# Two pairs of heads turned by transposing transfers instead of TensorE, in a MoBA attention and GELU MLP kernel

## The chip, the cores and the metric

The kernel runs on one core of a Trainium2 chip. A core has a matmul engine (TensorE; PE in the profile, and PEld for its loads of weights), three engines for elementwise work (VectorE: DVE; ScalarE: ACT; GpSimd: POOL) and SyncE (SP), which here does nothing but issue transfers. Each engine runs its own list of instructions in order and waits on semaphores for what others produce. The metric is device time in microseconds (us) for one execution, and lower is better.

## What is computed

```python
# q, k, v: (4, 8, 768, 64) f32; blocks of 64 positions, 12 blocks, top 3
k_rep = k.reshape(B, H, 12, 64, D).mean(axis=3)
gate = einsum('bhsd,bhnd->bhsn', q, k_rep)      # later blocks: -1e9
# each row sees its own block and the 3 blocks with the highest gates
scores = where(mask & causal, q @ k.T / 8, -1e9)
attn = softmax(scores)
x = (attn @ v)  ->  (4 * 768, 8 * 64)           # tokens x model
h = x @ w_in                                    # (3072, 512) @ (512, 2048)
out = gelu_tanh(h) @ w_out                      # (2048, 512) -> (3072, 512) f32
```

## The kernel before

**Work and stages.** All matmuls take fp16 operands. The 8 heads of a batch are handled in pairs: `HP = 4` pairs per batch, 16 pairs in all, and pair `p` belongs to batch `p // 4`. For a pair, `load` fetches k, q and v through SyncE's queue (the first piece as one operation, the others as a second one). `pre(p)` turns k and q so that the head dimension lies on partitions (for `p >= 4` a DVE stream transpose, L585), computes the gates (TensorE, L699), picks the three best blocks (DVE, L715 to L736) and puts the mask's rows beside q. Up to pair 7 TensorE turns the mask; from pair 8 on a transposing transfer on SyncE does so (L776). `heads(p)` then computes scores (L1059), exponentials (ACT, L1072), the causal cut (POOL, L1086), the product with v (L1098), and a division by the row sum (`norm`, DVE, L981 and L982) that writes the fp16 tile `xn` with tokens on partitions. There are three `xn` buffers. Batch 0 has a form of its own, `heads2`.

For the MLP a batch's attention output must lie with the model dimension on partitions, in `xT2[b % 2]`, one row of 128 partitions for each pair. That is the work of `turn_out(p)`, and it has two forms:

- **by TensorE**: six 128x128 transposes (`ot_e`, L1001) into one PSUM bank, and one copy from there into `xT2` (`otc_e`, through `copy`: L365 where ACT runs it, L369 where DVE does);
- **by transfer**: one `dma_start_transpose` on SyncE (`ot_dma`, L1006) from `xn` into `xT2`, with no other engine.

Before the change the second form is used by pairs 6, 8, 9, 10, 12, 13 and 14, the first one by all others. The last pair of each batch (3, 7, 11, 15) is always turned by TensorE.

Per batch, `s1` expands (L1135, GELU at L1147) and a second stage contracts: batch 0 plainly (`s2_plain`, L1335), the later batches by a seven-product scheme (`s2`, L1385, with sums at L1322 and joins at L1434 on DVE). The last batch also has a seven-product expansion (`s1_seven`, L1224). The stages overlap: while TensorE contracts batch 0, it also runs the heads of batch 1 and the preparation of batch 2, and so on.

**What sets the order.** The body builds a list of operations with `add`: the engines that may run each, its emitter, and what it depends on. Three tables written out in the file then decide the schedule. `ORDER` is the sequence in which operations are emitted, so that each engine's list is the part of `ORDER` that belongs to it. `BUFFER` picks the buffer for each operation that takes one. `ENGINE` holds the exceptions to "the first engine named". Nothing is reordered afterwards: SyncE's queue in particular is in order, so a transfer that waits for its data holds back the loads, masks and stores queued behind it.

**Fillers.** `warm` has 72 small matmuls on zeros (L1537) that compute nothing; `ORDER` contains 34 of them, most in the first microseconds.

Of the kernel before, what the change touches and what calls it, by code (L numbers as in the profile page):

```python
# [181 lines left out]
    "DVE": [  # L182
        2, 56, 61],
    "POOL": [
        338, 586, 587, 646, 647, 707, 708, 972, 973, 1035, 1036, 1097, 1098,
        1159, 1160, 1426, 1488, 1550, 1551]}


# [1451 lines left out]
```

## Time and profile before

| | us |
|---|---|
| median of 3 runs | 251.6 |
| the runs | 251.35, 251.6, 251.69 |
| the profiled execution, its own time | 252.62 |
| its span in the profile | 250.9 |
| PE busy | 245.2 |
| PEld busy | 170.7 |
| DVE busy | 194.9 |
| ACT busy | 173.8 |
| POOL busy | 82.2 |

The profiled execution is 1.0 us above the median of the runs, and 1.7 us of its time lies outside the span. Its mean granted TensorE clock was 0.997. Engine busy times are those of one profiled execution. Matmuls are pipelined, so one matmul's recorded duration overlaps the next one's, and a busy PE isn't PE at its peak. In rows of the timeline the columns are: start, duration, engine, line, operation, output and input, and xN for N instructions in a row.

### The profile page before, as it was taken

To read this page: it belongs to the slowest core of one execution; us is meant where nothing else is said; L and a number is where in the kernel's file an instruction comes from. 1 tells how busy PE (TensorE), PEld (TensorE's weight loads), DVE (VectorE), ACT (ScalarE), POOL (GpSimd) and SP (SyncE) were. 2 spreads that over 40 slices of the span, in tenths; PEclk is the share of its full clock that TensorE was granted. 3 is DMA by queue.
4 is the path that set the end of the run, shared out by engine and by line. 5 is a ranking of instruction groups with operands and counts; after the bars stand their busy time and mean duration, and the time that the engine had idled before them with its cause. 6 is when DMAs were issued, how large, how long until landed. Compare 5 with 4: busy or idle time off the path is not lost.

```text
span 250.9 us, 6484 instructions
## 1 busy us (share of the span) xinstructions
PE 245.2 (98%) x2504; PEld 170.7 (68%) x2504; DVE 194.9 (78%) x551; ACT 173.8 (69%) x220; POOL 82.2 (33%) x161
## 2 busy tenths in 40 slices
PE   8999999999999999999999999999999999999993
PEld 6768686555555666555788887656777887666883
DVE  3799971060989899999997999999788587788944
ACT  2788886635699997779997885586899932667200
POOL 8466660001147485080156351400256600000000
PEclk9999999999999999999999999999999999999998
DMA  6997899999897828999999486105813430020023
GB/s 181 229 203 158 138 210 186 211 172 161 156 172 125 160 47 153 177 234 195 205 191 186 74 155 109 26 3 135 206 44 37 108 114 0 3 84 0 3 105 146
DMA packets 128878, 32.61 MB, mean 130 GB/s; under 512 B 121456, under 2 KB 124880, under 8 KB 128848
## 3 DMA queue, kind: packets, MB, share of 16 engines
q1 hardware_dynamic: 125136, 27.62, 54.9%
q0 software_dynamic: 3136, 4.19, 9.9%
q10 hardware_dynamic: 576, 0.39, 0.6%
q8 instruction: 19, 0.31, 0.5%
q14 instruction: 11, 0.09, 0.2%
HBM read 27.26 MB, written 6.29 MB: 134 GB/s over the span
## 4 chain that ended last, share of the span: by engine, by line
PE 94%; DVE 4%; issue 0%; DVEq 0%
PE wide L1135 27%; PE bank L1385 22%; PE wide L1059 11%; PE bank L1335 8%; PE bank L1098 6%; PE wide L1224 6%; PE wide L876 3%; PE bank L699 2%; PE bank L1537 2%; PE bank L944 2%; PE bank L1001 1%; PE bank L565 1%; PE bank L558 1%; PE bank L769 1%; DVE sel L731 1%; DVE sel L722 1%
## 5 line engine op out<-in xcount | busy, mean ns | idle before, releaser
L1135 PE MATMUL wide<-xT,w_in 128*128 128x384 f16 x416 | 75.0, 326 | 0.0
L1072 ACT ACTIVATE ats<-wide 128x896 f16<-128x896 f32 x72 | 62.3, 915 | 5.9 <-PE wide L1059 4.6
L1147 ACT ACTIVATE G<-wide 128x768 f16<-128x768 f32 x52 | 41.8, 808 | 28.2 <-PE wide L1135 25.8
L1135 PEld LDWEIGHTS <-w_in 128*128 128x128 f16 x416 | 39.8, 98 | 25.9 <-issue 0.8
L1086 POOL TENSOR_SCALAR_AFFINE_SELECT ats<-ats 128x256 f16<-128x256 f16 x72 | 31.4, 448 | 64.6 <-ACT ats L1072 61.8
L1059 PE MATMUL wide<-qT,kT 76*128 76x512 f16 (+3 forms) x192 | 38.4, 305 | 0.0
L1385 PE MATMUL bank<-w_out,G 128*128 128x256 f16 x216 | 33.7, 272 | 0.0
L1385 PEld LDWEIGHTS <-G 128*128 128x128 f16 x288 | 26.7, 98 | 6.4
L585 DVE STREAM_TRANSPOSE s<-sd 128x768 f32<-128x768 f32 x24 | 23.3, 973 | 9.3 <-DMA sd<-in_k_dram 8.8
L1335 PE MATMUL bank<-w_out,G 128*128 128x512 f16 x96 | 29.2, 379 | 0.0
L1098 PEld LDWEIGHTS <-ats 128*128 128x128 f16 x504 | 22.7, 98 | 4.5 <-issue 0.3
L1434 DVE TENSOR_TENSOR osb<-bank,osb 128x512 f32<-128x512 f32 (+1 forms) x38 | 22.2, 594 | 4.4 <-PE bank L1385 3.0
L1098 PE MATMUL bank<-v,ats 128*128 128x65 f16 x504 | 24.9, 194 | 0.0
L1059 PEld LDWEIGHTS <-kT 76*128 76x128 f16 x192 | 17.3, 97 | 10.4 <-issue 0.6
L895 ACT ACTIVATE ats<-wide 128x1024 f16<-128x1024 f32 (+3 forms) x24 | 20.9, 919 | 3.1 <-PE wide L876 3.1
L1385 PEld LDWEIGHTS <-XS 128*128 128x128 f16 x216 | 20.1, 97 | 4.2 <-DVE XS L1322 0.2
L1385 PE MATMUL bank<-TS,XS 128*128 128x256 f16 x144 | 22.1, 272 | 0.0
L367 POOL CAST v<-vsd 128x768 f16<-128x768 f32 x12 | 10.3, 863 | 31.9 <-DMA vsd<-in_v_dram 31.8
L367 POOL CAST kT<-s 64x768 f16<-64x768 f32 x19 | 16.3, 862 | 9.3 <-DVE s L585 8.0
L982 DVE TENSOR_TENSOR xn<-bank,zr 128x384 f16<-128x384 f32 x24 | 13.4, 558 | 0.8
L731 DVE MAX8 sel<-sel 128x8 f32<-128x12 f32 x160 | 13.3, 157 | 0.6
L365 ACT CAST qT<-s 64x768 f16<-64x768 f32 x15 | 12.4, 825 | 0.2
(126 smaller groups left out, 356.2 us busy)
## 6 DMA issues: line engine op xcount, KB each, us to landing
out_dram<-osb SPq DMA_DIRECT2D x23, 256.0 KB
vsd<-in_v_dram SPq DMA_DIRECT2D x26, 192.0 KB
sd<-in_k_dram SPq DMA_DIRECT2D x48, 96.0 KB
sd<-in_q_dram SPq DMA_DIRECT2D x48, 96.0 KB
w_in<-in_moe_w_in_dram POOLq DMA_DIRECT2D x2, 1024.0 KB, 11.2
w_out<-in_moe_w_out_dram POOLq DMA_DIRECT2D x2, 1024.0 KB, 13.5
G<-in_k_dram SPq DMA_DIRECT2D x4, 192.0 KB
G<-in_q_dram SPq DMA_DIRECT2D x4, 192.0 KB
```

Of the source, the lines that this page charges most:

```text
L367: nc.gpsimd.tensor_copy(out=out, in_=in_)
L585: nc.vector.transpose(out=T[key + "T32", p], in_=T[key, p].rearrange("p t j -> p (t j)"))
L895: nc.scalar.activation(out=T["at", u][:, :, 0:n], in_=plan.buf[("st",) + u].rearrange("p (h w) -> p h w", h=2)[:, :, 0:n], func=AF.Exp, bi ...
L1059: nc.tensor.matmul(st[:, x:e], kT16[i][h][0:76, s0:s0 + 128], qT16[i][h][0:76, s0 + (x - cb):s0 + (e - cb)], start=True, stop=True)
L1072: nc.scalar.activation(out=T["at", u][:, 0:n], in_=plan.buf[("st",) + u][:, 0:n], func=AF.Exp, bias=0.0, scale=SCALE)
L1086: nc.gpsimd.affine_select(out=dg, in_=dg, compare_op=ALU.is_ge, fill=0.0, base=0, pattern=[[0, 2], [1, 128]], channel_multiplier=-1)
L1098: nc.tensor.matmul(pvv[:, qc, 0:65], at[:, cb + (qc - jc) * 128: cb + (qc - jc + 1) * 128], v16[i][:, jc, h, :], start=(gi == 0 and jc == ...
L1135: nc.tensor.matmul(hps[:, 512 * e:512 * e + HALF], w_in16[:, ci, (2 * j + e) * 128: (2 * j + e + 1) * 128], T["xT", b][:, ci, HALF * h:HAL ...
L1147: nc.scalar.activation(out=G[:, :, h, j, :], in_=plan.buf["hps", b, j, h].rearrange("p (e w) -> p e w", e=2)[:, :, 0:HALF], func=AF.Gelu_a ...
L1335: nc.tensor.matmul(plan.buf["ops", b, ti], G[:, f % 2, 2 * ti // NC, f // 2, ti % (NC // 2) * 128:ti % (NC // 2) * 128 + 128], w_out16[:, ...
L1385: nc.tensor.matmul(dst[:, HD * h:HD * h + HD], FACT[m][0][:, j, t * 128:(t + 1) * 128], FACT[m][1][:, j, :], start=(clear and j == 0), sto ...
L1434: nc.vector.tensor_tensor(out=dst(), in0=src(), in1=other(), op=ALU.add)
```

## The change

The condition in `turn_out` now admits all pairs of batch 1 but its last, so that pairs 4 and 5 take the second form too. The three tables were searched anew for this program. Because a turn by transfer adds three operations to the list where the turn by TensorE adds two, operation numbers shift by one behind pair 4's turn and by two behind pair 5's; the tables are therefore wholly replaced.

```diff
@@ turn_out @@
-        if p >= HP + 2 and hp != HP - 1:
+        if p >= HP and hp != HP - 1:
             go = add({SP: 1.3}, ot_dma, norms, -50)
             x = [add({"DMA": 0.8}, lambda _: None, [go], base - 20,
                      lag=2.0)] * 2
@@ ORDER, around the turns of pairs 4, 5 and 6 @@
...
-    662, 517, 665, 678, 715, 707, 663, 713, 714, 518, 579, 643, 519, 679,
...
-    1033, 673, 970, 685, 627, 527, 736, 724, 528, 628, 529, 743, 1036, 739,
...
+    686, 725, 737, 687, 974, 733, 529, 627, 1036, 530, 741, 730, 1026, 706,
+    531, 579, 688, 532, 738, 734, 745, 726, 544, 1027, 628, 739, 533, 689,
...
@@ ORDER, the last warm matmuls (1922 up to 1925) @@
...
-    1922, 784, 548, 1045, 785, 796, 1158, 786, 825, 450, 549, 826, 827, 828,
...
-    1098, 852, 1923, 853, 1473, 1002, 854, 821, 990, 1003, 487, 855, 856,
...
+    305, 1924, 1925, 294, 163, 317, 310, 326, 318, 306, 319, 328, 295, 153,
+    363, 364, 329, 311, 365, 315, 366, 358, 320, 356, 367, 324, 359, 149,
...
```

In the old numbers 579 and 627 are pair 4's and pair 5's transposes on TensorE, 580 and 628 the copies behind them (pair 4's on DVE, pair 5's on ACT), and 687 pair 6's transfer. In the new numbers 579, 628 and 689 are the transfers of pairs 4, 5 and 6; 627 and 688 are the second divisions of pairs 5 and 6, so pair 6's first and pair 5's second division change places on DVE. 1026 and 1027 are the two load operations of pair 9's q. SyncE's list around them, read out of the two tables:

| before | after |
|---|---|
| q of pair 9, first piece | q of pair 9, first piece |
| q of pair 9, others | **turn of pair 4** |
| q of pair 10, first | q of pair 9, others |
| k of pair 10, first | **turn of pair 5** |
| turn of pair 6 | turn of pair 6 |
| q of pair 10, others | k of pair 10, first |
| k of pair 11, first | q and k of pair 11, first |
| k of pair 10, others | q of pair 11, others |
| q of pair 11, first | v of pair 9, first |
| v of pair 9, first | k of pair 10, others |
| k of pair 11, others | an output store |
| v of pair 8, first | k of pair 11, others |
| v of pair 9, others | q of pair 10, first |
| mask of pair 8 | an output store |
| | q of pair 10, others |
| | v of pair 8, first |
| | mask of pair 8 |

The number of warm matmuls stays at 34. Before, two of them (1922 and 1923) lie in the expansion of batch 1; after, all of them stand ahead of the first expansion matmul of batch 0 (363). Operations that change their engine: in the first 36 us several copies, casts and turns move between DVE, ACT and POOL, in both directions, and ACT's first table load moves behind ACT's first loads and its first copy; in the last batch's expansion and contraction four copies and one sum move from DVE to ACT.

More of the change, by code (lines that the diff above doesn't have):

```diff
@@ L21 @@
 ORDER = [
[128 rows of a table removed]
-BUFFER = [
[23 rows of a table removed]
[128 rows of a table added]
+BUFFER = [
[23 rows of a table added]
 ENGINE = {
     "ACT": [
[4 rows of a table removed]
[5 rows of a table added]
     "DVE": [
-        2, 56, 61],
+        5, 56, 145],
     "POOL": [
-        338, 586, 587, 646, 647, 707, 708, 972, 973, 1035, 1036, 1097, 1098,
-        1159, 1160, 1426, 1488, 1550, 1551]}
+        337, 587, 588, 648, 649, 709, 710, 974, 975, 1037, 1038, 1099, 1100,
+        1161, 1162, 1427, 1428, 1552, 1615]}
 class Op:
```

303 rows, old and new, of tables (BUFFER, ENGINE, ORDER) are left out of this document.

## The prediction

> **What bounds the kernel now.** I read the busy times and the chain's shares first, to find the engine, then busy times by stretch, to see where that engine is without a gap, then the waits in the stretch where the two turns lie.
>
> ```profile
> span 250.9 us, 6484 instructions
> PE 245.2 (98%) x2504; PEld 170.7 (68%) x2504; DVE 194.9 (78%) x551; ACT 173.8 (69%) x220; POOL 82.2 (33%) x161
> ...
> PE 94%; DVE 4%; issue 0%; DVEq 0%
> ```
>
> TensorE is busy for 98% and is 94% of the chain. A share over the whole span doesn't say where work taken from it is worth its time, so here are four stretches (columns: length; busy time and instructions of PE, PEld, DVE, ACT, POOL; granted clock; DMA share; GB/s): batch 0's attention, the contraction of batch 0 with the heads of batch 1 in it, the expansion of batch 1, and the last batch's expansion.
>
> ```profile
> 0.00:36.00 36.00, 34.24 (x525) 25.63 (x526) 28.57 (x124) 26.70 (x37) 24.01 (x56) 1.00 0.92 186
> 62.00:98.50 36.50, 36.50 (x395) 21.60 (x395) 32.36 (x101) 32.72 (x42) 20.14 (x37) 1.00 0.77 134
> 98.50:121.00 22.50, 22.50 (x156) 13.11 (x155) 21.85 (x81) 17.62 (x24) 5.10 (x6) 1.00 0.98 198
> 204.00:231.00 27.00, 26.97 (x189) 18.25 (x188) 21.41 (x32) 14.89 (x18) 0.00 (x0) 1.00 0.10 40
> ```
>
> Up to 36 us TensorE has 1.76 us of gaps. In the second stretch, where pairs 4 and 5 are turned, and in the third it has none, and the clock is full. Idle time of DVE there (4.14 of 36.50) is nobody's bound. Of the waits in 62.00 to 98.50, TensorE itself has no row; its loads of weights have seven, first and last:
>
> ```profile
> PEld bank L699 <- issue: 0.7, 2, 0.4
> ...
> PEld L1001 <- DVE xn L982: 0.3, 1, 0.3
> ```
>
> Such a load waits while the matmul before it still runs, so none of them opens a gap. The end is set by how much TensorE has to issue behind the first stretch; what leaves its list there should come off the end, if nothing else becomes late.
>
> **Part 1: twelve transposes leave TensorE.** Pair 4's and pair 5's, with the matmul behind each:
>
> ```profile
> 86.01 0.50 PE L1001 MATMUL bank<-ident,xn 128*128 128x128 f16 x6
> 86.34 0.38 PE L1335 MATMUL bank<-w_out,G 128*128 128x512 f16 x1
> ...
> 91.96 0.50 PE L1001 MATMUL bank<-ident,xn 128*128 128x128 f16 x6
> 92.29 0.81 PE L1335 MATMUL bank<-w_out,G 128*128 128x512 f16 x3
> ```
>
> The recorded 0.50 overlaps the matmul that follows, so the cost in the stream is from start to start: 86.34 − 86.01 = 0.33, and 92.29 − 91.96 = 0.33. Both lie in a stretch without gaps: **−0.66 us**, bounded above by the recorded 2 × 0.50 = 1.00 and below by nothing, if the gap is filled by another wait.
>
> **Part 2: two copies go, three transposing transfers now stand in one row on SyncE.** All tiles written into `xT2`, grouped (count: shortest/median/longest in ns, first and last start):
>
> ```profile
> L369 DVE COPY xT<-bank x7: 349/551/558, 31.9 to 203.2; 128x768 f16<-128x768 f16 x5, 128x384 f16<-128x384 f16 x2
> L1006 SPq DMA_TRANSPOSE xT<-xn x7: 1212/1377/2127, 93.0 to 199.4; - x7
> L365 ACT COPY xT<-bank x3: 793/798/799, 92.8 to 154.0; 128x768 f16<-128x768 f16 x3
> ```
>
> A copy of 0.55 leaves DVE and one of 0.80 leaves ACT. Both engines have more idle time than that between 62.00 and 98.50, so I cost these at nothing: they are slack for others, not path. Each new transfer takes SyncE 1.2 to 2.1 us, median 1.38. Where do they fit? SyncE's list around the turn of pair 6, and the third of the last four divisions of pairs 5 and 6 (DVE, L982), which is pair 6's first in the old order and pair 5's second in the new one:
>
> ```profile
> 84.38 2.92 SPq L411 DMA_DIRECT2D sd<-in_q_dram  x5
> 87.34 0.76 SPq L411 DMA_DIRECT2D sd<-in_k_dram  x1
> 92.97 1.34 SPq L1006 DMA_TRANSPOSE xT<-xn  x1
> 94.36 1.70 SPq L411 DMA_DIRECT2D sd<-in_q_dram  x3
> ...
> 103.77 1.36 SPq L776 DMA_TRANSPOSE mT<-madd  x1
> ```
> ```profile
> 90.75 0.56 DVE L982 TENSOR_TENSOR xn<-bank,zr 128x384 f16<-128x384 f32 x1
> ```
>
> SyncE issues nothing from 87.34 + 0.76 = 88.10 to 92.97: it waits for pair 6's second division. Pair 4's data is complete before 86.01, when it is turned today; its transfer comes behind the first of the loads that begin at 84.38 and doesn't wait. Pair 5's second division, third in the new order, ends at 90.75 + 0.56 = 91.31; its transfer then takes 91.31 to about 92.69, and pair 6's can start at 92.97 as before. So the two new transfers fill a hole of 4.87 us in SyncE's list, and pair 6's turn isn't delayed by issue time.
>
> Are they in time? The expansion of batch 1 reads the four pairs in turn:
>
> ```profile
> 95.85 0.49 PE L1135 MATMUL wide<-xT,w_in 128*128 128x384 f16 x2
> ...
> 98.54 0.65 PE L1135 MATMUL wide<-xT,w_in 128*128 128x384 f16 x3
> ```
>
> Pair 4's row is needed at 95.85, some 9 us behind its issue; pair 5's at about 97, 5.7 behind; pair 6's no earlier than 98.54. TensorE waits for nothing there today, so pair 6's transfer, issued at 92.97, has landed within 98.54 − 92.97 = 5.6 us or a little more. With at most that for pair 5's, it lands by 91.31 + 5.6 = 96.9, which is just when it is needed, and this is an upper bound. Cost taken: 0.
>
> The wait of pair 5's turn holds back what is queued behind it on SyncE: pair 6's turn and then the first pieces of pair 10's k, pair 11's q and pair 11's k, three more of q 11, and so on; pair 10's q moves to the end of that row. Nothing on TensorE waits directly; DVE's stream transposes (L585) do. Its first use of that row today is at
>
> ```profile
> 99.97 0.97 DVE L585 STREAM_TRANSPOSE s<-sd 128x768 f32<-128x768 f32 x1
> ```
>
> and takes pair 10's q, whose last pieces were issued by 94.36 + 1.70 = 96.06: 3.9 us ahead. In the new order pair 11's q takes that place; its last piece is the sixth behind pair 6's turn, at 1.70 / 3 = 0.57 each: 94.36 + 6 × 0.57 = 97.8, which leaves 2.2 us, 1.7 less. The other three of the group keep more than 4 us, worked out in the same way. DVE didn't wait for a load at that place, so landing takes at most 3.9 us; how much less the trace of before doesn't show. I take 0 and price the other case below.
>
> **Part 3: two warm matmuls leave the expansion of batch 1** (they go ahead of 36 us, where TensorE has gaps).
>
> ```profile
> 109.84 0.27 PE L1537 MATMUL bank<-XS 128*128 128x256 f16 x1
> 109.95 0.33 PE L1135 MATMUL wide<-xT,w_in 128*128 128x384 f16 x1
> ...
> 121.74 0.27 PE L1537 MATMUL bank<-XS 128*128 128x256 f16 x1
> ```
>
> Start to start 0.11, twice: **−0.22 us**, and the two take 0.22 us of the 1.76 us of gaps in the first stretch.
>
> **Part 4: other engines for some copies and a table load, at the two ends.** In the first stretch two of the moves bear on TensorE's gaps.
>
> ```profile
> 1.76 1.28 ACT L842 ACT_TABLE_LOAD   x1 [1.76 <-PEq L1624]
> ...
> 5.97 0.68 ACT L365 COPY s<-bank 128x384 f32<-128x384 f32 x1 [2.72 <-PE bank L565]
> 7.45 1.71 ACT L365 CAST XS<-bank 128x384 f16<-128x384 f32 x2 [0.80 <-DVE ks L604]
> ```
> ```profile
> 21.54 1.01 DVE L369 COPY s<-bank 128x384 f32<-128x384 f32 x2
> ```
>
> The two copies at 21.54 (1.01 us) go from DVE to ACT; if DVE's chain sets the first stretch, that is worth up to −1.0. The table load (1.28) goes behind the copy that ends at 5.97 + 0.68 = 6.65; it then ends at 7.93, while the casts behind it start at 7.45 today: up to +0.5. I take 0, between the two, since each needs its engine to be the bound at that place and the chain has only 4% of DVE. In the last batch's expansion DVE has 21.41 and ACT 14.89 of 27.00, so a few copies moved from one to the other fit in either: 0, within ±0.5.
>
> **Sum.** −0.66 − 0.22 = −0.88 us. Against the profiled execution's own 252.62: 251.7. That execution was 1.0 us above the median of the runs shown; the edits don't depend on what made it so, and 251.6 − 0.9 = **250.7 us** for the median.
>
> **The rivals.**
> - *The gain is given back.* The first stretch costs up to 0.5 and the last expansion up to 0.5, and together they eat the 0.88: **251.6**. For it: all three tables are different, and parts outside the turns are moved. Against: both places have idle time on the engines that get more. The Trainium skill's "Perfetto Trace Analysis", in Identifying the Most-Contended Engine, says that matmul busy time is a poor measure of TensorE's headroom and that the busy share of weight loads is the better one. By that rule 68% would be slack, and the gain 0. The trace speaks against it at this place: starts follow each other without a gap, and no row names TensorE as waiting.
> - *Slower: loads held back on SyncE.* Pair 11's q is issued 1.7 us closer to its stream transpose. If landing takes the full 3.9 us, DVE stands still for 1.7 us at about 100 us, in a stretch where it is busy for 21.85 of 22.50 and can make up only 0.65; what it prepares there are the masks and sums of batch 1's contraction. It decides once a landing takes longer than 2.2 us by more than that 0.65. Undiminished on TensorE, it costs 1.7: 250.7 + 1.7 = **252.4**. For it: DVE's share there, and a DMA share of 0.98. Against: DVE's list is also in a new order, and some of its work could be done first.
> - *Slower by far: the transfers run one after another.* If the 5.6 us of pair 6's turn are transfer time and not latency, and the queue does one at a time, pair 5's would run 91.31 to 96.9 and pair 6's 96.9 to 102.5, while it is needed from 98.54 on, at about 98.9 (one matmul later): 3.6 us late, 250.7 + 3.6 = **254.3**. Against: SyncE starts a new piece 1.4 us behind a turn, and the 5.6 is only an upper bound. The Trainium skill's "VectorE: DVE Perf Modes" speaks for it, and against the change: under The three transpose paths and Rules for kernel authors it gives 1309 ns for 128x128 by DMA against 390 ns on TensorE, and advises TensorE wherever PSUM will do as a destination. By it six blocks would take 7.9 us, an estimate from that page; the trace disagrees, since 5.6 us were enough for pair 6's six.
> - *The order also shortens the first stretch*, by the 1.0 us of part 4: **249.7**.
>
> **How the numbers follow.** The forecast (250.7, own range 250.2 to 251.2, from ±0.5 at either end of the kernel) gets 0.55, since it needs only that work leaves an engine without gaps. Gain given back: 0.17. Loads late: 0.18. Transfers in series: 0.04. Shorter first stretch: 0.06. A run of this kernel can tell 0.2% or 0.5 us from no change. Faster by more: 0.53 of the forecast's 0.55 and the last rival's 0.06, 0.59; the same: 0.17 and the 0.02 left, 0.19; slower: 0.22. The range 249.8 to 252.4 reaches to the late loads and leaves out the transfers in series and half of the last rival's cases.
>
> **What the changed profile would show.** Right: six transposes by TensorE in seven groups instead of nine, nine L1006 transfers, three of them between 85 and 95 us; no wait of TensorE between 62 and 121 us; PE busy down by about 0.7 to 0.9; the first expansion matmul (L1135) still at about 36.5. Part 4 is wrong if that first L1135 moves by more than 0.3. The late loads would show as DVE idle before L585, released by a DMA, at about 100 us, and as PE busy below its stretch between 98 and 145 us. Transfers in series would show as a gap of TensorE before L1135 near 98 us, released by a DMA into xT. The forecast is wrong if PE loses its 0.9 us and the end doesn't move: then the rows of waits between 121 and 250 us must show who gave it back.

## The result, and the profile after

| | before | after |
|---|---|---|
| median, 12 runs of each | 251.83 us | 251.3 us |
| lowest and highest | 251.35 to 252.4 | 250.97 to 251.91 |
| the profiled execution, its own time | 252.62 | 251.68 |
| its span | 250.9 | 250.0 |

The ratio of after to before is 0.9977, 95% interval 0.9966 to 0.9987: the change is faster by 0.53 us of the medians, where 0.88 was forecast. A second set of 12 runs of the same kernel (e8 below) gave 251.25 and a ratio of 0.9975 (0.9959 to 0.999).

The page of the profile after, its span, busy times and chain:

```profile
span 250.0 us, 6442 instructions
PE 244.1 (98%) x2492; PEld 170.0 (68%) x2492; DVE 189.0 (76%) x542; ACT 178.1 (71%) x226; POOL 81.0 (32%) x162
...
PE 90%; DMA 5%; DVE 3%; ACT 0%; issue 0%; POOL 0%; DVEq 0%
```

Twelve matmuls fewer, and something new in the chain: 5% of a DMA. The busy times by stretch (columns as in the prediction; the second row, from 36 to 62 us, is the expansion of batch 0) say where it is. The kernel before in that second stretch, and then the changed kernel in all four:

```profile
36.00:62.00 26.00, 26.00 (x182) 15.37 (x179) 5.96 (x11) 14.82 (x20) 2.46 (x4) 1.00 1.14 184
```
```profile
0.00:36.00 36.00, 34.24 (x527) 25.48 (x527) 27.98 (x122) 27.71 (x39) 23.79 (x57) 1.00 0.92 183
36.00:62.00 26.00, 25.64 (x185) 14.94 (x183) 5.29 (x10) 14.31 (x19) 2.51 (x4) 1.00 1.16 186
62.00:98.50 36.50, 36.50 (x383) 21.67 (x376) 34.41 (x103) 33.16 (x42) 20.03 (x37) 1.00 0.78 139
98.50:121.00 22.50, 22.50 (x166) 13.54 (x165) 20.56 (x79) 16.51 (x23) 3.94 (x4) 1.00 1.03 203
```

From 62 us on TensorE still has no gap. Between 36 and 62 it lost 0.36 us that it did not lose before. Its timeline at the first contraction matmul, before and after:

```profile
46.27 0.81 PE L1135 MATMUL wide<-xT,w_in 128*128 128x384 f16 x4
46.92 0.38 PE L1335 MATMUL bank<-w_out,G 128*128 128x512 f16 x1
```
```profile
44.60 0.65 PE L1136 MATMUL wide<-xT,w_in 128*128 128x384 f16 x3
45.61 0.38 PE L1336 MATMUL bank<-w_out,G 128*128 128x512 f16 x1 [0.36 <-DMA w_out<-in_moe_w_out_dram]
45.83 0.48 PE L1136 MATMUL wide<-xT,w_in 128*128 128x384 f16 x2
```

The first contraction matmul has ten expansion matmuls fewer ahead of it than before (48 instead of 58). It wants to start at 45.25 and waits for the first half of w_out. Before, it started at 46.92 without a wait.

The turns. SyncE's list, and the tiles written into `xT2`:

```profile
86.80 1.33 SPq L1007 DMA_TRANSPOSE xT<-xn  x1
88.19 1.70 SPq L412 DMA_DIRECT2D sd<-in_q_dram  x3
92.13 2.76 SPq L1007 DMA_TRANSPOSE xT<-xn  x2
94.95 0.57 SPq L412 DMA_DIRECT2D sd<-in_k_dram  x1
95.57 0.52 SPq L412 DMA_DIRECT2D sd<-in_q_dram  x1
96.13 0.52 SPq L412 DMA_DIRECT2D sd<-in_k_dram  x1
96.70 1.66 SPq L412 DMA_DIRECT2D sd<-in_q_dram  x3
```
```profile
L1007 SPq DMA_TRANSPOSE xT<-xn x9: 1209/1211/1330, 86.8 to 198.9; - x9
```

Nine transfers, three of them ahead of batch 1's expansion, which begins at 96.07; pair 4's runs without waiting, pair 5's waits for its division until 92.13, pair 6's follows at once. TensorE waits for none of them, and its transposes are down from 54 to 42, as forecast.

For the accounting I use two landmarks of each trace: the start of the first expansion matmul, and the time from there to the last matmul's start. Before they are 36.51 and 210.22, after 36.30 and 209.65. Each ratio in the table is to runs of the kernel before that were timed beside that kernel; their medians were 251.81 to 251.93.

| kernel | median | ratio to before (95%) | first expansion matmul | from there to the last matmul |
|---|---|---|---|---|
| before | 251.83 | | 36.51 | 210.22 |
| after | 251.3 | 0.9977 (0.9966 to 0.9987) | 36.30 | 209.65 |
| e1_turns_only | 251.7 | 1.0001 (0.9987 to 1.0014) | 35.63 | 209.89 |
| e2_order_only | 252.13 | 1.0012 (1.0 to 1.0024) | 35.55 | 210.33 |
| e3_contract_later | 250.95 | 0.997 (0.9957 to 0.9984) | 35.91 | 209.29 |
| e4_ten_warm | 252.52 | 1.0032 (1.002 to 1.0045) | 36.28 | 210.39 |
| e5_turns_filled | 251.25 | 0.9977 (0.9963 to 0.9992) | 35.24 | 209.81 |
| e6_two_more_turns | 263.32 | 1.0457 (1.0432 to 1.0482) | 42.48 | 215.34 |
| e7_pair7_turn | 251.5 | 0.9984 (0.997 to 0.9997) | 35.60 | 210.08 |
| e8_changed_again | 251.25 | 0.9975 (0.9959 to 0.999) | 36.19 | 209.13 |
| e9_two_fillers_off | 250.59 | 0.9947 (0.9928 to 0.9967) | 35.63 | 209.14 |
| e10_contract_later_again | 250.87 | 0.9961 (0.9947 to 0.9974) | 36.17 | 209.30 |
| e11_old_two_fillers_off | 251.4 | 0.9982 (0.9967 to 0.9996) | 35.37 | 210.13 |

The last column repeats closely: the part of it from batch 2's expansion on is 97.59 or 97.60 in all four kernels in the old order, and 96.22 or 96.23 in all nine in the new one. (The new order has done more of TensorE's work by then, so this difference isn't a gain.) The column before it does not repeat. Kernels with the same first stretch differ: 35.24 to 36.51 in the old order (before, e1, e5, e11), 35.55 to 36.30 in the new one. Profiles taken on one chip differ as well (e2, e3 and e4: 35.55, 35.91, 36.28). That is most of the scatter of the times, and an effect of 0.2 us is therefore read from the last column and only then looked for in the medians.

The traces show two places where this scatter arises. One is the start. TensorE's first 36 matmuls on real data, in the kernel before and in e11, whose order is the same up to the first expansion:

```profile
4.38 3.50 PE L565 MATMUL bank<-identk,G 128*64 128x128 f32 x36
```
```profile
4.38 2.65 PE L564 MATMUL bank<-identk,G 128*64 128x128 f32 x36
```

Neither row has a gap. In the first, these matmuls come in pairs 0.21 us apart until 7.0 us and 0.11 apart from there on; in the second they are 0.11 apart from 4.5 us on. So TensorE begins an execution at half its later rate, and across the thirteen profiles the full rate came between 3.8 and 7.0 us.

The other place is near 15 us. VectorE adds two tiles for the gates while GpSimd casts a v that has just landed. In the changed kernel, and in e2, which has the same order there:

```profile
15.49 0.93 DVE L723 TENSOR_TENSOR sel<-sel,cgate 128x120 f32<-128x120 f32 x1
15.46 0.83 POOL L368 CAST v<-G 128x768 f16<-128x768 f32 x1 [0.34 <-DMA G<-in_v_dram]
18.04 0.45 PE L770 MATMUL bank<-ident,madd 128*128 128x128 f16 x5 [0.63 <-DVE madd L737]
```
```profile
15.24 0.28 DVE L722 TENSOR_TENSOR sel<-sel,cgate 128x120 f32<-128x120 f32 x1
15.32 0.89 POOL L367 CAST v<-G 128x768 f16<-128x768 f32 x1 [0.45 <-DMA G<-in_v_dram]
```

Where the cast starts ahead of the add (after, e4, e8, e10), the add takes 0.76 to 0.93 us, to about the end of the cast, and TensorE stands still for 0.47 to 0.63 us ahead of the next mask's transposes. Where the cast starts behind it (the other five profiles in the new order), the add takes 0.28 and TensorE has no such wait. The first expansion matmul is at 36.17 to 36.30 in the first four and at 35.55 to 35.91 in the others but e6. In the old order the profile of before alone has this, later: an add of 0.91 at 26.59, behind a cast that starts at 26.55, and a wait of 0.44 at 29.12.

### The profile page after: what moved, and what is told of

Same layout as the page of the kernel before. It is cut to its first block, busy times and chain, and to the rows that moved or that the text cites. A ratio compares the mean times of both kernels' runs of the same rounds, so it can differ in the third digit from the quotient of the medians.

```text
span 250.0 us, 6442 instructions
## 1 busy us (share of the span) xinstructions
PE 244.1 (98%) x2492; PEld 170.0 (68%) x2492; DVE 189.0 (76%) x542; ACT 178.1 (71%) x226; POOL 81.0 (32%) x162
## 4 chain that ended last, share of the span: by engine, by line
PE 90%; DMA 5%; DVE 3%; ACT 0%; issue 0%; POOL 0%; DVEq 0%
PE wide L1136 24%; PE bank L1386 22%; PE wide L1060 11%; PE bank L1336 8%; PE bank L1099 6%; PE wide L1225 6%; DMA w_out<-in_moe_w_out_dram 5%; PE wide L877 2%; PE bank L700 2%; PE bank L1538 2%; PE bank L566 2%; PE bank L945 2%; PE bank L770 1%; PE bank L559 1%; DVE ks L605 1%; DVE sel L732 1%
## 5 line engine op out<-in xcount | busy, mean ns | idle before, releaser
L1136 PE MATMUL wide<-xT,w_in 128*128 128x384 f16 x416 | 74.2, 326 | 0.0
L1087 POOL TENSOR_SCALAR_AFFINE_SELECT ats<-ats 128x256 f16<-128x256 f16 x72 | 30.8, 438 | 57.5 <-ACT ats L1073 56.9
L1386 PE MATMUL bank<-w_out,G 128*128 128x256 f16 x216 | 31.6, 272 | 0.0
L1336 PE MATMUL bank<-w_out,G 128*128 128x512 f16 x96 | 27.3, 379 | 0.4 <-DMA w_out<-in_moe_w_out_dram 0.4
L1099 PEld LDWEIGHTS <-ats 128*128 128x128 f16 x504 | 21.8, 98 | 3.8 <-POOL v L368 0.2
L1099 PE MATMUL bank<-v,ats 128*128 128x65 f16 x504 | 23.8, 194 | 0.0
L1386 PE MATMUL bank<-TS,XS 128*128 128x256 f16 x144 | 21.6, 272 | 0.0
L366 ACT CAST qT<-s 64x768 f16<-64x768 f32 x18 | 14.8, 824 | 0.2
L368 POOL CAST v<-vsd 128x768 f16<-128x768 f32 x13 | 11.4, 880 | 10.2 <-DMA vsd<-in_v_dram 10.1
```

Of the source, the lines that this page charges most:

```text
L368: nc.gpsimd.tensor_copy(out=out, in_=in_)
L1087: nc.gpsimd.affine_select(out=dg, in_=dg, compare_op=ALU.is_ge, fill=0.0, base=0, pattern=[[0, 2], [1, 128]], channel_multiplier=-1)
L1099: nc.tensor.matmul(pvv[:, qc, 0:65], at[:, cb + (qc - jc) * 128: cb + (qc - jc + 1) * 128], v16[i][:, jc, h, :], start=(gi == 0 and jc == ...
L1136: nc.tensor.matmul(hps[:, 512 * e:512 * e + HALF], w_in16[:, ci, (2 * j + e) * 128: (2 * j + e + 1) * 128], T["xT", b][:, ci, HALF * h:HAL ...
L1336: nc.tensor.matmul(plan.buf["ops", b, ti], G[:, f % 2, 2 * ti // NC, f // 2, ti % (NC // 2) * 128:ti % (NC // 2) * 128 + 128], w_out16[:, ...
L1386: nc.tensor.matmul(dst[:, HD * h:HD * h + HD], FACT[m][0][:, j, t * 128:(t + 1) * 128], FACT[m][1][:, j, :], start=(clear and j == 0), sto ...
```

## The experiments

**e1: the turns alone, in the old order.**

```diff
-        if p >= HP + 2 and hp != HP - 1:
+        if p >= HP and hp != HP - 1:
 ORDER of before, renumbered; the two copies left out
-    ..., 518, 579, 519, ... 580, ... 627, 527, 528, 628, ...
+    ..., 518, 579, 519, ...      ... 627, 527, 528, ...
```

> The kernel before with its own order, buffers and engines; only the turns of pairs 4 and 5 go by transfer, at the places where TensorE's transposes stood (pair 4's ahead of the last piece of pair 7's v, pair 5's ahead of pair 6's), and the two copies are gone. Theory (the slots of TensorE are worth their time): 0.66 us less than before, a ratio of 0.997; last matmul 0.66 earlier, first expansion matmul unmoved at 36.5. Rival (the gain of the changed kernel comes from its new order, the slots were covered): ratio 1.000.

The last column fell by 0.33, half of what was expected, and the median by nothing that can be told. TensorE's timeline of e1:

```profile
85.55 0.38 PE L1334 MATMUL bank<-w_out,G 128*128 128x512 f16 x1
86.14 0.54 PE L1058 MATMUL wide<-qT,kT 76*128 76x512 f16 x2 [0.20 <-ACT ats L1071]
86.51 0.44 PE L768 MATMUL bank<-ident,madd 128*128 128x128 f16 x5
```

and the same scores in the kernel before:

```profile
86.77 0.38 PE L1335 MATMUL bank<-w_out,G 128*128 128x512 f16 x1
87.02 0.54 PE L1059 MATMUL wide<-qT,kT 76*128 76x512 f16 x2
```

These scores wait for an exponential to free one of the two wide PSUM buffers. A contraction matmul occupies the stream for 0.22, so they could have started at 85.77 and start at 86.14: 0.37 lost. Before, pair 4's transposes stood 0.7 us ahead of them (their slot ends at 86.34), and the scores followed the matmul ahead of them by 0.25, nearly its own 0.22. Pair 4's slot had been covering this wait; pair 5's was worth the rest, about its 0.33.

**e2: the new order alone**, pairs 4 and 5 on TensorE again.

```diff
-        if p >= HP and hp != HP - 1:
+        if p >= HP + 2 and hp != HP - 1:
 ORDER of after, old numbers; transposes 579 and 627, copies 580 (DVE) and 628 (ACT) put back
+    ..., 579, 520, ... 580, 613, ... 627, 530, ... 628, 725, ...
```

> The changed kernel's order, buffers and engines, but pairs 4 and 5 turned by TensorE and a copy again (pair 4's between two contraction matmuls near 87 us, pair 5's near 92.5 us). Theory: 0.66 us more than the changed kernel's 251.3, so 252.0, and a ratio of about 1.000 to before: what the new order gives (0.22 for two fillers, 0.2 in the first stretch) the wait for w_out takes back (0.36). Rival (the order makes the gain): 251.3, ratio 0.998.

252.13, as the theory had it, and 0.83 above the changed kernel. Its last column holds two things that e8's doesn't: 0.39 of wait for w_out (its first contraction starts at 44.73, 9.18 behind the first expansion matmul, where e8's starts 8.79 behind), and 0.16 at 68 us that some executions in the new order have ahead of a gate matmul (e3, e4, e7 and e10 too; after, e6, e8 and e9 not; the gates' operands are fp32, not fp16 as the text on the kernel before has it for all matmuls). Without them it is 209.78, 0.65 more than e8's 209.13. In the new order both slots of 0.33 come through in full; which of its moves takes away the wait that e1 met was not tested.

**e3: the first contraction later.**

```diff
 ORDER of after
-    ..., 376, 433, 393, 394, 395, 396, 434, ...
+    ..., 376, 393, 394, 395, 396, 433, 434, ...
```

> The changed kernel with its first contraction matmul (which waits 0.36 us for w_out at 45.25) behind four more expansion steps, just ahead of the second one, at about 46.5 us. Theory: the wait for w_out is what keeps the changed kernel from the forecast: 0.36 us less than the changed kernel, 250.9, a ratio of 0.9964 to before, and no wait of TensorE for w_out. Rival (the time comes back at another wait behind it, or the transfer then ends later too): 251.3, ratio 0.998.

250.95 was measured, TensorE has no wait for w_out, and the last column is 0.36 shorter than in the changed kernel's first profile. That this is the 0.36 of the theory is luck: it is the 0.52 that the wait cost from start to start, less the 0.16 at 68 us, which this profile has and the changed kernel's doesn't. And e8 below shows that the wait isn't there in each execution.

**e4: ten more fillers in the expansion of batch 1.**

```diff
 ORDER of after: one of 1926 ... 1935 ahead of every fifth expansion step of batch 1
+    ..., 1926, 770, ... 1927, 755, ... 1935, 804, ...
```

> The changed kernel with ten more filler matmuls in the expansion of batch 1 (98 to 120 us); they compute nothing. Theory (TensorE has no slack there, a filler costs its start-to-start time of 0.11): 1.1 us more, 252.4, a ratio of 1.002 to before. Rival (TensorE's busy time hides slack, the wait moves elsewhere): under 0.3 us more than 251.3.

252.52: 1.2 us more. The last column is 1.26 above e8's; less the 0.16 at 68 us that is 1.10, ten times 0.11 to the digit. TensorE has no slack in that stretch.

**e5: other work in pair 4's place, in the old order.**

```diff
 ORDER of e1
-    ..., 520, 684, 719, 521, ... 522, ...
+    ..., 520, 521, 522, 684, 719, ...
```

> The kernel before with pairs 4 and 5 turned by transfer (as in e1_turns_only), and two contraction matmuls that stood just behind the scores at 86 us now ahead of them. In e1 the time from the first expansion matmul to the last matmul fell by 0.33 us (210.22 to 209.89) where the two slots are 0.66, and those scores waited for an exponential on ScalarE. Theory (pair 4's slot was cover for that wait, and other work in its place lets the gain through): 209.56, no wait there, 0.66 us less than before. Rival (ScalarE sets the pace of this stretch, and the wait moves to the next scores): 209.89 again.

The last column is 209.81, 0.08 less than e1's: the rival was nearly right. The wait at 86 is gone, and another 0.20 opens ahead of the scores at 88.38. ScalarE's timeline of e5 says why:

```profile
84.78 5.16 ACT L1071 ACTIVATE ats<-wide 128x896 f16<-128x896 f32 x6 [0.48 <-PE wide L1058]
```

Six exponentials stand back to back. ScalarE sets the pace of these scores in the old order, so a slot taken from TensorE here is returned at the next score. The median, 251.25, is 0.45 below e1's, which 0.08 doesn't explain. The intervals of the two ratios overlap, though barely; the first expansion matmul is 0.39 earlier in e5's profile with the same first stretch, so I read this as the scatter of that stretch.

**e6: two more turns by transfer, beside the weights.**

```diff
-        if p >= HP and hp != HP - 1:
+        if hp != HP - 1 and p != 2:
 ORDER of e3: copies 227 and 261 left out, fills 153 and 149 ahead of the turns on SyncE
```

> e3_contract_later with pairs 0 and 1 of batch 0 also turned by transfer, queued behind the fills and ahead of the hold on SyncE, while the weights are on their way; two slots of TensorE and two copies of VectorE fewer before the first expansion. Theory (a turn lands some 2.5 us behind its issue wherever it is): the first expansion matmul up to 0.66 us earlier, 250.3 to 250.9. Rival (beside the weights' transfers the turn lands late): the first expansion matmuls wait for a transfer into xT, and the time is at or above e3's 250.95.

Twelve us slower. The waits of e6 between 20 and 50 us, the rows that concern the turns, and then the two turns on SyncE and the first instruction that each one holds up:

```profile
DVE xn L963 <- DMA xT<-xn: 7.1, 1, 7.1
PEld L1001 <- DVE xn L963: 6.8, 1, 6.8
PE bank L1001 <- DVE xn L963: 6.7, 1, 6.7
...
PE wide L1135 <- DMA xT<-xn: 3.4, 1, 3.4
```
```profile
26.87 1.47 SPq L1006 DMA_TRANSPOSE xT<-xn  x1
30.28 4.74 SPq L1006 DMA_TRANSPOSE xT<-xn  x1
...
41.57 0.56 DVE L963 TENSOR_TENSOR xn<-bank,zr 128x384 f16<-128x384 f32 x1 [7.11 <-DMA xT<-xn]
...
46.78 0.80 PE L1135 MATMUL wide<-xT,w_in 128*128 128x384 f16 x2 [3.45 <-DMA xT<-xn]
```

There are three `xn` buffers. Pair 3's division wants the buffer of pair 0, which the transfer has not yet finished reading: VectorE waits 7.1 us, TensorE 6.7 for VectorE, and then 3.4 more for pair 1's row. Pair 0's turn was issued at 26.87 and its buffer came free at 41.57, 14.7 us later; pair 1's was issued at 30.28 and its row could be read at 46.78, 16.5 us later, while w_in and w_out moved. What in the DMA engines makes it so long was not separated; e7 shows that the same transfer is far shorter elsewhere. While TensorE stood still, the clock that it was granted fell: its mean was 0.66 from 36 to 42 us, 0.50 from 42 to 47 and 0.71 from 47 to 55, so the expansion matmuls behind the waits were slow too.

**e7: the last pair of batch 1 by transfer too.**

```diff
-        if p >= HP and hp != HP - 1:
+        if p >= HP and (hp != HP - 1 or p == 7):
 SyncE's list of e3: pair 7's turn between k of pair 11, first, and q of pair 11, others
```

> e3_contract_later with pair 7, the last of batch 1, also turned by transfer, as soon as its second division is done (about 97 us); TensorE has one slot fewer and reads the row about 1.2 us later. It measures the time from a turn's issue to its data, of which the kernel before only showed that it is under 5.6 us. If that time is 2.4: TensorE waits about 1.2 us for a transfer into xT, 0.9 us more than e3, 251.8. If it is 5.6: a wait of 4.4, 255. If it is under 1.2: no wait, 250.6.

The turn was issued at 96.07 (SyncE), and TensorE's timeline shows when it could read it:

```profile
96.07 1.21 SPq L1006 DMA_TRANSPOSE xT<-xn  x1
```
```profile
96.53 1.14 PE L1135 MATMUL wide<-xT,w_in 128*128 128x384 f16 x6
98.64 0.48 PE L1135 MATMUL wide<-xT,w_in 128*128 128x384 f16 x2 [0.97 <-DMA xT<-xn]
```

98.64 − 96.07 = 2.57 us from issue to use. The wait costs 1.14 start to start (98.64 less 96.53 + 6 × 0.163), the slot saved is 0.33, and the last column is 0.79 above e3's. In this kernel the last three pieces of pair 11's q are issued at 97.32, 2.30 behind the start of the expansion instead of 0.63, and nothing more is lost.

**e8: the changed kernel again.** No edit.

> The changed kernel once more, beside the others on the same chip. Theory (what is behind the first expansion matmul is the same in each execution, and the scatter between executions comes from the first 36 us): 209.1 to 209.7 us from the first expansion matmul to the last matmul, the spread by the wait for w_out alone; the first expansion matmul anywhere from 35.5 to 36.5; ratio 0.9977 again. Rival: the later part scatters as well, by 0.3 us or more beside the wait for w_out.

The part behind the first expansion matmul is 209.13: 209.65 less 0.52, which is what the wait for w_out cost from start to start (45.61 where the stream without it gives 45.09). e8 has no such wait:

```profile
44.33 0.81 PE L1136 MATMUL wide<-xT,w_in 128*128 128x384 f16 x4
44.98 0.38 PE L1336 MATMUL bank<-w_out,G 128*128 128x512 f16 x1
45.20 0.98 PE L1136 MATMUL wide<-xT,w_in 128*128 128x384 f16 x5
```

The first contraction starts 8.79 us behind the first expansion matmul here, 9.31 in the first profile. It arrives together with its weights, so it waits or doesn't as the load and the first stretch fall out. Four profiles have the first contraction at this place: the changed kernel's first one lost 0.52 there and e2 0.39, e8 and e4 nothing.

**e9 and e10: the last two fillers off, beside e3 again.**

```diff
 ORDER of e3
-    305, 1924, 1925, 294, 163, ...
+    305, 294, 163, ...
```

> e3_contract_later without the last two fillers, which in the changed kernel stand 1.5 us ahead of the first expansion matmul, in a row of matmuls without a gap, and compute nothing. Theory (moving the two fillers from the expansion of batch 1 to there moved their 0.22 us, it didn't save them): 0.22 us less than e3, by the median and by the first expansion matmul; 209.1 to 209.3 us from there to the last matmul. Rival (the first 36 us have gaps that cover them, as forecast): the same time as e3.

> e3_contract_later once more, beside e9 on the same chip. Theory (the wait for w_out is there in some executions only, since it was in one of two profiles of the changed kernel): 251.0, up to 0.3 us less than the changed kernel's 251.25 to 251.3; 209.1 to 209.3 us from the first expansion matmul to the last, with no wait for w_out. Rival (always there): 250.75, 0.5 us less.

e10 gave 250.87 and e9 250.59, 0.28 less; their intervals overlap, and the trace says the rest. TensorE ahead of the first expansion matmul, in the changed kernel:

```profile
34.44 0.55 PE L945 MATMUL bank<-v,ats 128*128 128x65 f16 x12
34.83 0.38 PE L1538 MATMUL bank<-XS 128*128 128x256 f16 x2
35.05 0.50 PE L1002 MATMUL bank<-ident,xn 128*128 128x128 f16 x6
```

and in e9:

```profile
33.92 0.55 PE L944 MATMUL bank<-v,ats 128*128 128x65 f16 x12
34.38 0.49 PE L1001 MATMUL bank<-ident,xn 128*128 128x128 f16 x6
...
35.63 0.65 PE L1135 MATMUL wide<-xT,w_in 128*128 128x384 f16 x3
```

From the start of the twelve matmuls with v to the first expansion matmul it is 1.86 with the fillers (34.44 to 36.30) and 1.71 without (33.92 to 35.63): they cost 0.15 there, in a row without gaps. The other profiles with the fillers, e6 aside, have the same 1.86. The last column is unmoved but for the 0.16 at 68 us. e10's profile has the wait near 18 us and e9's doesn't, so the medians may differ by more than the fillers. e10 against the changed kernel's two sets is 0.4 less, between theory (0.3) and rival (0.5); its interval reaches from 0.9947 to 0.9974, so how often the wait for w_out is there stays open.

**e11: the old order without its two fillers** in the expansion of batch 1.

```diff
 ORDER of before
-    1922, 784, ...      852, 1923, 853, ...
+    784, ...            852, 853, ...
```

> The kernel before without the two fillers in the expansion of batch 1, nothing else changed. Theory (TensorE has no gap there): 210.22 minus 2 x 0.11 = 210.00 us from the first expansion matmul to the last matmul, ratio 0.999. Rival (slack there): 210.22.

The last column is 210.13: 0.09 less, not 0.22. So of the forecast's 0.22 less than half is seen in the old order. Sixteen gate matmuls near 114 us now take 0.80 us up to what follows them (113.34 to 114.14) where they took 0.68 (114.59 to 115.27 before): 0.12 came back there. The median is 0.41 lower, with an interval from 0.9967 to 0.9996 that holds anything from 0.1 to 0.8 us.

## Why the prediction was right, and where not

The direction was right, 251.3 lies in the range, and 0.53 us of the 0.88 forecast came. Point by point:

- **Part 1, −0.66 for twelve transposes.** Right in the new order: 0.65 between e2 and e8. But the reason given, that the stretch has no gap and so whatever leaves it comes off the end, was too simple. In the old order (e1) only 0.33 came, since work in a stretch without gaps can cover a wait that opens when it leaves. A gapless engine proves that its work is needed only where no other engine keeps the same pace; ScalarE did, with six exponentials back to back in e5. The bound "below by nothing, if the gap is filled by another wait" held this case.
- **Part 2, the transfers cost nothing.** Right. 5.6 us from issue to data was an upper bound; e7 measured 2.57, so pair 5's row, issued at 92.13 (0.8 later than worked out), was there well ahead of its use. "Transfers in series", priced at 5.6 us for each transfer, falls by the same number, and with it the advice of the Trainium skill's "VectorE: DVE Perf Modes", Rules for kernel authors, to turn 128x128 on TensorE, for this place: a pair costs 2.57 us of latency that nobody waits for, against 0.33 of the engine that sets the end. At e6's place, where a turn took 14.7 and 16.5 us, the advice holds by far.
- **"Loads held back".** Wrong as a danger. The last piece of pair 11's q was issued by 98.36, later than the 97.8 worked out, but VectorE's new list turns it at 104.61 and not at 99.97. From 62 to 121 us neither VectorE nor TensorE waited for a load of q or k. e7 issued it 1.67 us later still, reckoned from the expansion's start, without a loss.
- **Part 3, −0.22 for two fillers.** This step failed. It said that the fillers' new place is covered by gaps of the first stretch. The gaps are there (1.76 us, as before), but not at that place: the fillers stand in a row without a gap, 1.5 us ahead of the first expansion matmul. They were moved, and e9 shows that 0.15 of their 0.22 is paid at the new place. What counts is where a gap lies, not how much of it a stretch has.
- **A term that was missing.** The first contraction matmul was moved ten expansion matmuls forward, into the landing of w_out: 0.52 and 0.39 us in two of the four profiles that have it there. It could have been read from the two orders and the 46.92 of the old trace, if the place of each weight's first use had been compared; the prediction followed SyncE's and VectorE's lists and not this one. e3 and e10 (0.3 to 0.4 us less than the changed kernel) fit, without settling its mean.
- **Part 4, nothing from the first stretch.** Not settled for the copies and the table load, which the scatter of this stretch hides; the means of the first expansion matmul are 35.69 over the four profiles in the old order and 36.00 over the seven in the new order with fillers and without e6's turns. What the traces do show is a wait that the prediction didn't look for: 0.5 to 0.6 us near 18 us, in four of the nine profiles in the new order and in both of the changed kernel's, when GpSimd's cast starts just ahead of VectorE's add.
- **"Gain given back".** Part of the gain was given back: to the wait for w_out, the fillers' new place and the wait near 18 us. The rival named the first stretch as a place, and none of these reasons. The Trainium skill ("Perfetto Trace Analysis", Identifying the Most-Contended Engine) judges TensorE's headroom by the busy share of weight loads, along with a second measure. That share is 13.54 of 22.50 us, or 60%, in the stretch where e4 puts its ten fillers; read as room to spare it would make them free, and e4 measured 1.10 us for them. (The prediction calls 68% slack; that is the busy share, and 32% would be slack.)

The account: 0.66 for the turns and 0.22 for the fillers, with 0.21 more that other moves behind 36 us gave, make 1.09 from 210.22 to e8's 209.13. The 0.21 is what remains over; it was traced to no single move. Of the 1.09 about 0.15 go back ahead of the first expansion matmul (e9), up to 0.52 into the wait for w_out, and 0.5 to 0.6 into the wait near 18 us where it occurs; 0.53 and 0.68 were measured. How often the two waits occur is known from a few profiles only, so this is consistent with the medians and doesn't prove them. That the forecast was off by no more than 0.35 is in part luck: an unforeseen gain stands against unforeseen waits.

e9, the changed kernel with the first contraction later and two fillers fewer, is the fastest kernel here: 250.59 us, a ratio of 0.9947 (0.9928 to 0.9967) to before.

## What to carry to other kernels

Where one engine runs without a gap, price an instruction that leaves it from start to start, and then look at what follows within the next microsecond: if that needs a buffer that another engine frees only just in time, the slot was cover and some of its time comes back as a wait. An instruction moved elsewhere is saved only if its new place has a gap there, which a sum of gaps over a stretch does not say. When an order is replaced as a whole, compare for each large load the place of its first use with its landing.

## What the runs showed of the hardware

A transposing transfer of a 128x768 fp16 tile took 2.57 us from issue to use in a stretch where the DMA share is 0.78 (e7), and 14.7 and 16.5 us while 4 MB of weights were on their way (e6): the same instruction is free in one stretch and the bound in another. An fp32 add of VectorE on 128x120 took 0.28 us, and 0.76 to 0.93 when a cast on GpSimd had started up to 0.2 us ahead of it. TensorE ran at half its later rate until 3.8 to 7.0 us into an execution. With the last two, the first 36 us of one order end up to 1.3 us apart between executions, while the last 97 us repeat to 0.01.
